# Loads of batch 1 ahead of its bits, and the output weights in two other slots, in a hash attention with SwiGLU on one Trainium2 core

## The chip, the cores and the metric

One NeuronCore of a Trainium2 chip runs the whole program. The metric is the device time of one execution in microseconds (us). A measurement gives several executions; their median is quoted, and one more execution is profiled.

## The reference: what is computed

Four batches of eight heads attend over 768 tokens of 64 numbers. A query sees only the keys whose six hash bits equal its own. The result goes, without a residual, through an RMS norm and a SwiGLU layer.

```python
q_bits = (einsum('bhsd,dk->bhsk', q, proj) > 0);  k_bits = (einsum(..., k, proj) > 0)
mask = q_bucket[:, :, :, None] == k_bucket[:, :, None, :]
scores = where(mask, scale * q @ k.T, -1e9)
attn = exp(scores - max);  attn = attn / (sum(attn) + 1e-9)
x = (attn @ v) laid out as 3072 tokens x 512
xn = x / sqrt(mean(x * x) + 1e-6) * rms_g
g, val = xn @ w_gate, xn @ w_val          # 512 x 1536 each
out = (g * sigmoid(g) * val) @ w_out      # 1536 x 512
```

## The kernel before, in words

**Tiles.** Heads are taken in pairs: (b, hp) is pair hp of batch b. The queries of a batch are halved, so that there are eight windows w of 384 queries, two to a batch. One score tile is one window, one head and a third of the keys (256): two matmuls of 128 keys by 384 queries in `scores` (L344). SLOTS (L35) lists the 192 of these tiles; slot s of the program prepares the scores of tile s + 1 and does the rest of what is due. Tiles 0 to 47 belong to batch 0, 48 to 95 to batch 1. The mask costs no instruction of its own: twelve rows of hash bits, with signs and weights, stand below the 64 rows of k and of q in the tile QK, so that one matmul adds the mask to the scores, and ACT's exp (L354) brings masked ones to zero.

**How a pair is prepared.** Its k, q and v come by DMA into tiles kL, qL and vL of a pool of ten buffers (`lpool`). In batch 0 and pair (1,0), k and q come as rows (`load_rows`, L112) and are turned by PE. In all other pairs they come as blocks (`load_blocks`, L122): four DMAs for k and four for q, each of 24 x 32 x 32 numbers in runs of 128 bytes. DVE turns them with four transposes each (L194, `turn_dve`), POOL casts them into QK (L202), PE multiplies them with the projection (L210, `d_ps`), DVE takes the signs (L217, `bits`), and DMAs of SP carry the bits into QK: eight DMAs for (1,0) (L268) and eight for each of (1,1) to (1,3) (L285); L303 does it for two pairs of later batches at a time. v is cast by POOL (L310) and summed by POOL (L316 to L318, `v_sum`).

**The feed-forward part.** When a window's eight heads are done it is normalised, turned (L431), multiplied by the gate weights (L446) and the value weights (L456), and by the output weights wo (L469, `project`). For window 0 the gate matmuls begin in slot 42 and the project matmuls in slot 58: slot 58 uses row blocks 0 to 3 of the twelve of wo, slot 59 blocks 4 to 7. The weights come by DMAs that POOL issues and that turn fp32 into fp16: gate and value weights in halves (L520), wo in two halves of six row blocks (`load_wo`, L526).

**What sets the order.** Everything is ordered by hand. `at(s, f, ...)` (L576) puts a step into slot s; inside a slot, steps go by rank and then in the order in which they were put there. The dictionary `work` (L636) gives for each pair the slots of its k, q and v load, the first of its eight turning slots and the slot of its hash. The casts follow four and eight slots after the first turn, v's cast and sum nine after it. A slot says only where an instruction stands in its engine's queue. SP's queue holds nothing but DMA issues: loads, bits and the stores of the result (L478). SP goes through it in order, and an issue that has to wait, for data or for an earlier DMA, holds all that stand behind it. POOL's queue holds the weight loads among its arithmetic.

**What the loads wait for.** Each load needs a free buffer of the ten, and each of SP's DMAs waits for the one eight places before it on the queue. The matmuls that make g_ps, v_ps, y_ps, x_ps, t_ps, m_ps and d_ps share three PSUM banks (`bank`, tag "g"), taken in the order of the program.

Of the kernel before, what the change touches and what calls it, by code (L numbers as in the profile page):

```python
# [44 lines left out]
def kernel(  # L45
# [530 lines left out]
    def at(s, f, *a, rank=3):  # L576
        plan[s].append((rank, len(plan[s]), lambda: f(*a)))
# [36 lines left out]
    for i, (t, src) in enumerate(((wg, moe_w_gate), (wv, moe_w_val))):  # L614
        at(2 + 4 * i, load_w, t, src, 0, 768)
        at(12 + 9 * i, load_w, t, src, 768, 1536)
        at(43 + 7 * i, load_wo, 6 * i, 6 * i + 6)


    for which, sl in zip("kqv", (9, 11, 15)):  # L620
# [12 lines left out]
    def in_row(loads, s, hash_slot=None):  # L633
        return loads, range(s, s + 8), (s + 4, s + 8, s + 9), hash_slot

    work = {  # L636
        (1, 1): in_row((21, 32, 33), 42, 51), (1, 2): in_row((38, 42, 44), 49, 58),
        (1, 3): in_row((46, 52, 54), 56, 65),
        (2, 0): in_row((56, 60, 62), 64), (2, 1): in_row((63, 66, 69), 72, 81),
        (2, 2): in_row((71, 75, 78), 81), (2, 3): in_row((80, 83, 86), 89, 98),  # L640
        (3, 0): in_row((90, 94, 98), 100), (3, 1): in_row((100, 104, 108), 110, 119),
        (3, 2): in_row((116, 120, 124), 126), (3, 3): in_row((126, 130, 134), 136, 145),
    }
# [120 lines left out]
```

## Time and profile before

| what | us |
|---|---|
| median of 3 runs (340.05 to 343.66) | 341.2 |
| the profiled execution | 340.95 |
| its span, first to last instruction | 339.2 |
| PE busy | 326.1 |
| DVE busy | 237.7 |
| ACT busy | 207.9 |
| POOL busy | 155.6 |

The profile shows one execution. A row of its timeline has the start in us from the beginning of the span, the duration, the engine, the line of the kernel, the operation, the tiles (out<-in) and how many instructions are merged; in brackets stands the idle time of the engine ahead of it and what ended it. SPq is SP's queue of DMA issues: the duration is that of issuing, not of the transfer. A row of a table by stretch gives, for PE, PEld (weight loads), DVE, ACT and POOL, the busy us and the count, then PEclk, the share of full clock that TensorE was granted, the share of time that the 16 DMA engines were busy and the GB/s moved. Queue q1 carries the DMAs of SP, q0 those of POOL.

### The profile page before, as it was taken

What the parts mean: (1) busy time and instruction counts of PE and PEld (TensorE: products, weight loads), DVE (VectorE), ACT (ScalarE), POOL (GpSimd) and SP (SyncE); (2) the same over time, 40 slices, a digit from 0 to 9 for tenths busy, and PEclk for the clock granted to TensorE, in tenths of its full rate; (3) what the DMA queues carried; (4) which work ended last, traced back from release to release, by engine and by line L of the source; (5) the groups of instructions that cost most, each with busy time, mean ns of one, the idle gap of its engine ahead of it and who ended that gap; (6) DMA issues with size and microseconds to landing.
All of it is one profiled execution on the core that took longest, in us unless ns stands there. A gap on an engine that the chain in (4) does not pass through costs nothing.

```text
span 339.2 us, 7797 instructions
## 1 busy us (share of the span) xinstructions
PE 326.1 (96%) x2983; PEld 200.2 (59%) x2983; DVE 237.7 (70%) x532; ACT 207.9 (61%) x324; POOL 155.6 (46%) x230
## 2 busy tenths in 40 slices
PE   8999989599989999999999999999999999999995
PEld 7566666265555655656565655656566655655653
DVE  4789669489587986978767794977356754784860
ACT  3789987356465755666665766666666766532321
POOL 4888766178745586374826156463101311130000
PEclk9999999989999999999999999999999999999999
DMA  7998929947273947605531572000110001001002
GB/s 236 334 231 192 140 50 183 175 79 135 44 177 78 199 56 178 109 9 119 124 82 24 109 121 90 22 12 7 38 56 2 3 31 64 2 1 62 33 0 93
DMA packets 85972, 31.36 MB, mean 92 GB/s; under 512 B 71480, under 2 KB 82992, under 8 KB 85936
## 3 DMA queue, kind: packets, MB, share of 16 engines
q1 hardware_dynamic: 82000, 26.09, 33.4%
q0 software_dynamic: 3712, 4.72, 8.8%
q8 instruction: 23, 0.38, 0.5%
q14 instruction: 13, 0.11, 0.1%
q10 hardware_dynamic: 224, 0.07, 0.1%
HBM read 28.32 MB, written 6.29 MB: 102 GB/s over the span
## 4 chain that ended last, share of the span: by engine, by line
PE 80%; DVE 8%; POOL 3%; DMA 3%; SPq 2%; issue 2%; ACT 1%; DVEq 0%; ACTq 0%; POOLq 0%
PE y_ps L469 18%; PE v_ps L456 16%; PE s_ps L344 14%; PE g_ps L446 13%; PE o_ps L366 8%; PE d_ps L210 4%; PE s_ps L446 3%; DMA kL<-in_k_dram 2%; PE x_ps L431 1%; SPq L122 1%; SPq L285 1%; PE z_ps L337 1%; PE t_ps L170 1%; DMA QK<-bits 1%; DVE t L457 1%
## 5 line engine op out<-in xcount | busy, mean ns | idle before, releaser
L354 ACT ACTIVATE psb<-s_ps 128x768 f16<-128x768 f32 x192 | 150.6, 809 | 33.5 <-PE s_ps L344 31.7
L344 PE MATMUL s_ps<-QK 76*128 76x384 f16 x384 | 93.7, 326 | 3.0 <-DMA QK<-bits 1.3
L456 PE MATMUL v_ps<-xnT,wv 128*128 128x384 f16 x384 | 78.7, 327 | 0.0
L469 PE MATMUL y_ps<-wo,ht 128*128 128x512 f16 x276 | 69.2, 379 | 0.1
L448 ACT ACTIVATE t<-g_ps 128x384 f32<-128x384 f32 x78 | 38.2, 490 | 48.0 <-PE g_ps L446 47.5
L457 DVE SCALAR_TENSOR_TENSOR t<-t,g_ps 128x384 f32<-128x384 f32 x78 | 42.7, 547 | 32.5 <-ACT t L448 32.1
L366 PEld LDWEIGHTS <-psb 128*128 128x128 f16 x1152 | 52.4, 98 | 22.0 <-issue 3.9
L446 PE MATMUL g_ps<-xnT,wg 128*128 128x384 f16 x312 | 63.5, 325 | 1.2 <-DVE xnT L432 0.6
L390 POOL TENSOR_TENSOR x<-otmp,rcp 128x384 f32<-128x384 f32 x31 | 25.9, 835 | 83.6 <-DVE rcp L386 83.1
L458 DVE SCALAR_TENSOR_TENSOR ht<-t,v_ps 128x384 f16<-128x384 f32 x96 | 53.2, 554 | 10.8 <-PE v_ps L456 1.5
L366 PE MATMUL o_ps<-vl,psb 128*128 128x65 f16 x1152 | 56.9, 194 | 0.0
L446 PEld LDWEIGHTS <-wg 128*128 128x128 f16 x384 | 36.1, 97 | 25.2 <-issue 1.7
L456 PEld LDWEIGHTS <-wv 128*128 128x128 f16 x384 | 36.4, 98 | 23.8 <-issue 0.9
L344 PEld LDWEIGHTS <-QK 76*128 76x128 f16 x384 | 31.3, 98 | 20.8 <-issue 8.2
L469 PEld LDWEIGHTS <-ht 128*128 128x128 f16 x276 | 25.9, 97 | 25.1 <-issue 1.5
L476 ACT COPY ysb<-y_ps 128x512 f32<-128x512 f32 x23 | 13.5, 586 | 25.3 <-PE y_ps L469 24.9
L402 POOL TENSOR_TENSOR sq<-x 128x384 f32<-128x384 f32 x31 | 25.7, 827 | 2.5
L432 DVE TENSOR_TENSOR xnT<-x_ps,gcol 128x512 f16<-128x512 f16 x24 | 16.2, 681 | 14.5 <-PE x_ps L431 14.5
L202 POOL CAST QK<-qT 64x768 f16<-64x768 f32 x22 | 18.2, 827 | 17.2 <-DVE qT L194 16.5
L194 DVE STREAM_TRANSPOSE kT<-kL 128x192 f32<-128x192 f32 x44 | 22.1, 516 | 4.3 <-issue 4.3
L381 DVE TENSOR_TENSOR otmp<-o_ps,cvb 128x390 f32<-128x390 f32 x32 | 17.9, 558 | 8.1 <-PE o_ps L366 8.0
L202 POOL CAST QK<-kT 64x768 f16<-64x768 f32 x22 | 18.2, 828 | 10.5 <-PE v_ps L456 4.1
(80 smaller groups left out, 301.7 us busy)
## 6 DMA issues: line engine op xcount, KB each, us to landing
vL<-in_v_dram SPq DMA_DIRECT2D x16, 384.0 KB
out_dram<-ysb SPq DMA_DIRECT2D x23, 256.0 KB
kL<-in_k_dram SPq DMA_DIRECT2D x44, 96.0 KB
qL<-in_q_dram SPq DMA_DIRECT2D x44, 96.0 KB
kL<-in_k_dram SPq DMA_DIRECT2D x4, 384.0 KB
qL<-in_q_dram SPq DMA_DIRECT2D x4, 384.0 KB
wg<-in_moe_w_gate_dram POOLq DMA_DIRECT2D x2, 768.0 KB, 7.2
wv<-in_moe_w_val_dram POOLq DMA_DIRECT2D x2, 768.0 KB, 8.4
```

The costliest lines, as they stand in the source:

```text
L202: nc.gpsimd.tensor_copy(QK[b, hp][0:64, hh, o : o + S], T0[b, hp, which][64 * hh : 64 * hh + 64, :])
L344: nc.tensor.matmul(ps[:, j, 0:HALF], k_cols(w // 2, h, 2 * p + j), q_cols(w, h), start=True, stop=True,)
L354: nc.scalar.activation(psb[w, h][:, p], sps.pop(g)[:, :, 0:HALF], AF.Exp, scale=ESCALE,)
L366: nc.tensor.matmul(o[:, c, hh, 0:65], psb[w, h][:, jt // 2, jt % 2, 128 * c : 128 * c + 128], vls[b % 2][:, h, v_chunk(b, h, jt), 0:65], s ...
L390: eng.tensor_mul(xd.rearrange("p c (h d) -> p c h d", h=2), tmp[:, :, :, 0:64], r.to_broadcast([128, 3, 2, 64]),)
L402: nc.gpsimd.tensor_mul(sq, xd, xd)
L446: nc.tensor.matmul(g, wg[:, kt, fs], xnT[w][:, kt], start=(kt == 0), stop=(kt == 3))
L448: nc.scalar.activation(t, g, AF.Tanh, scale=0.5)
L456: nc.tensor.matmul(vv, wv[:, kt, fs], xnT[w][:, kt], start=(kt == 0), stop=(kt == 3))
L457: nc.vector.scalar_tensor_tensor(out=t, in0=t, scalar=1.0, in1=g, op0=ALU.add, op1=ALU.mult)
L458: nc.vector.scalar_tensor_tensor(out=ht[w][:, ft], in0=t, scalar=0.5, in1=vv, op0=ALU.mult, op1=ALU.mult)
L469: nc.tensor.matmul(y, ht[w][:, ft, c * 128 : (c + 1) * 128], wo[:, ft, :], start=(ft == 0), stop=(ft == NF - 1),)
```

## The change

Only numbers of slots change.

```diff
-        at(43 + 7 * i, load_wo, 6 * i, 6 * i + 6)
+        at(31 + 21 * i, load_wo, 6 * i, 6 * i + 6)
...
-        (1, 1): in_row((21, 32, 33), 42, 51), (1, 2): in_row((38, 42, 44), 49, 58),
-        (1, 3): in_row((46, 52, 54), 56, 65),
-        (2, 0): in_row((56, 60, 62), 64), (2, 1): in_row((63, 66, 69), 72, 81),
-        (2, 2): in_row((71, 75, 78), 81), (2, 3): in_row((80, 83, 86), 89, 98),
+        (1, 1): in_row((21, 22, 32), 42, 51), (1, 2): in_row((32, 33, 37), 49, 58),
+        (1, 3): in_row((38, 40, 44), 56, 65),
+        (2, 0): in_row((53, 55, 58), 64), (2, 1): in_row((59, 62, 66), 72, 81),
+        (2, 2): in_row((68, 71, 75), 81), (2, 3): in_row((78, 82, 86), 89, 98),
```

The three numbers in brackets are the slots of the k, q and v load. The turning slots and the hash slots stay. The order of the loads among themselves stays too, so each takes the same buffer as before. On PE, DVE and ACT no instruction moves. What moves is on SP and POOL.

On SP, from the k of (1,1) to the bits of (1,1), the order before:

```order
21 L122 DMA kL<-in_k_dram 32x24x32 x4
22 L268 DMA QK<-bits 12x384 x8
23 L122 DMA qL<-in_q_dram 32x24x32 x4
24 L112 DMA vL<-in_v_dram 128x2x384
25 L122 DMA kL<-in_k_dram 32x24x32 x4
26 L122 DMA qL<-in_q_dram 32x24x32 x4
27 L112 DMA vL<-in_v_dram 128x2x384
28 L122 DMA kL<-in_k_dram 32x24x32 x4
29 L285 DMA QK<-bits 12x384 x8
```

and now:

```order
21 L122 DMA kL<-in_k_dram 32x24x32 x4
22 L122 DMA qL<-in_q_dram 32x24x32 x4
23 L268 DMA QK<-bits 12x384 x8
24 L112 DMA vL<-in_v_dram 128x2x384
25 L122 DMA kL<-in_k_dram 32x24x32 x4
26 L122 DMA qL<-in_q_dram 32x24x32 x4
27 L112 DMA vL<-in_v_dram 128x2x384
28 L122 DMA kL<-in_k_dram 32x24x32 x4
29 L122 DMA qL<-in_q_dram 32x24x32 x4
30 L112 DMA vL<-in_v_dram 128x2x384
31 L285 DMA QK<-bits 12x384 x8
```

The q of (1,1) has moved ahead of the bits of (1,0) (L268), and the q and v of (1,3) ahead of the bits of (1,1) (L285).

On SP behind the bits of (1,1), up to the bits of (1,3), the order before:

```order
30 L122 DMA qL<-in_q_dram 32x24x32 x4
31 L112 DMA vL<-in_v_dram 128x2x384
32 L122 DMA kL<-in_k_dram 32x24x32 x4
33 L285 DMA QK<-bits 12x384 x8
34 L122 DMA qL<-in_q_dram 32x24x32 x4
35 L478 DMA out_dram<-ysb 128x512
36 L112 DMA vL<-in_v_dram 128x2x384
37 L122 DMA kL<-in_k_dram 32x24x32 x4
38 L478 DMA out_dram<-ysb 128x512
39 L285 DMA QK<-bits 12x384 x8
```

and now:

```order
32 L122 DMA kL<-in_k_dram 32x24x32 x4
33 L122 DMA qL<-in_q_dram 32x24x32 x4
34 L285 DMA QK<-bits 12x384 x8
35 L112 DMA vL<-in_v_dram 128x2x384
36 L122 DMA kL<-in_k_dram 32x24x32 x4
37 L478 DMA out_dram<-ysb 128x512
38 L122 DMA qL<-in_q_dram 32x24x32 x4
39 L478 DMA out_dram<-ysb 128x512
40 L285 DMA QK<-bits 12x384 x8
```

Ahead of the bits of (1,2) (the first L285 row) stand now k and q of (2,0), where q and v of (1,3) and the k of (2,0) stood. Between these bits and those of (1,3) are still eleven DMAs; the q of (2,1) is there instead of the q of (2,0).

On POOL, the second half of wo (slot 52 instead of 50), a piece of the difference behind the casts of (1,1):

```order
 L402 TENSOR_TENSOR sq<-x 128x384
 L202 COPY QK<-kT 64x768 x2
-L526 DMA wo<-in_moe_w_out_dram 128x6x512
 L202 COPY QK<-qT 64x768 x2
 L390 TENSOR_TENSOR x<-otmp,rcp 128x3x128
```

and where it stands now, behind the sum of the v of (1,1):

```order
 L317 TENSOR_TENSOR vadd<-vadd 128x2x64
 L318 TENSOR_TENSOR vsum_110<-vadd 128x2x64
+L526 DMA wo<-in_moe_w_out_dram 128x6x512
 L202 COPY QK<-kT 64x768 x2
 L415 TENSOR_SCALAR ms<-ss 128x3
```

It has moved from ahead of the q casts of (1,1) to ahead of the k casts of (1,2). The first half moves from slot 43 to 31, where it stands behind the last casts of (1,0) and ahead of the norm of window 0 (L415).

## The prediction

> **What bounds the kernel now.** I read the page's head first, then the waits of PE from 50 to 110 us, then PE and DVE side by side at the longest of them, then the DMA issues ahead of it. The head, and the waits (us in total, times, longest):
>
> ```profile
> span 339.2 us, 7797 instructions
> PE 326.1 (96%) x2983; PEld 200.2 (59%) x2983; DVE 237.7 (70%) x532; ACT 207.9 (61%) x324; POOL 155.6 (46%) x230
> ...
> PE d_ps L210 <- DVE t L457: 3.5, 1, 3.5
> PE s_ps L344 <- DMA QK<-bits: 1.3, 2, 1.1
> PE g_ps L446 <- DVE t L457: 0.5, 1, 0.5
> ```
>
> PE is the bound: 326.1 of 339.2 us. A change of loads alone can win only what PE idles, or loses to its clock, and can lose only by making PE wait. The matmuls on both sides of the longest wait, and DVE's work there:
>
> ```profile
> 62.44 0.81 PE L446 MATMUL g_ps<-xnT,wg 128*128 128x384 f16 x4
> 66.73 0.56 PE L210 MATMUL d_ps<-kT,pk 128*32 128x384 f32 x1 [3.48 <-DVE t L457]
> ...
> 60.92 0.52 DVE L194 STREAM_TRANSPOSE qT<-qL 128x192 f32<-128x192 f32 x1
> 65.77 0.52 DVE L194 STREAM_TRANSPOSE kT<-kL 128x192 f32<-128x192 f32 x1 [4.33 <-issue]
> ```
>
> PE stands 3.48 us because the bank for slot 51's hash comes free only with a DVE L457, and that stands behind DVE's transpose of the k of (1,2), slot 49, which waited 4.33 us. "Issue" means that the page shows no releaser; the operand's load is the one left. Busy time by stretch (PE, PEld, DVE, ACT, POOL; then PEclk, DMA share, GB/s):
>
> ```profile
> 52.00:60.00 8.00, 8.00 (x75) 5.06 (x74) 7.55 (x19) 6.03 (x11) 4.30 (x6) 1.00 1.10 185
> 64.00:72.00 8.00, 5.27 (x33) 2.56 (x34) 5.02 (x12) 2.06 (x4) 3.66 (x5) 0.79 0.91 162
> 60.00:84.00 24.00, 20.52 (x179) 11.41 (x178) 17.67 (x40) 12.20 (x20) 14.37 (x19) 0.93 0.77 134
> 102.00:110.00 8.00, 7.54 (x68) 4.84 (x69) 5.52 (x12) 4.42 (x8) 4.33 (x6) 1.00 0.38 79
> ```
>
> After standing, PE's clock is 0.79 over 8 us: 0.21 x 8 = 1.7 us of its work lost. So one late load costs 3.5 + 1.7 = 5.2 us. Why it is late: the issues of SP and of POOL, the time that the two wo loads took to land, and what SP's queue q1 moved between 59 and 65 us (packets, MB, share):
>
> ```profile
> 46.95 2.71 SPq L122 DMA_DIRECT2D qL<-in_q_dram  x4
> 49.76 0.59 SPq L112 DMA_DIRECT2D vL<-in_v_dram  x1
> 50.45 8.08 SPq L122 DMA_DIRECT2D kL<-in_k_dram  x4
> ...
> 49.12 0.94 POOL L526 DMA_DIRECT2D wo<-in_moe_w_out_dram  x1
> 57.72 0.89 POOL L526 DMA_DIRECT2D wo<-in_moe_w_out_dram  x1
> ...
> DMA to landing us min/median/max: 7.6/8.6/9.6
> ...
> q1 hardware_dynamic: 1751, 0.22, 32.9%
> ```
>
> The four DMAs of a block load are issued in 2.71 us undisturbed, but in 8.08 while wo is under way, from 49.12 to between 65.3 and 67.3. In 6 us of that q1 moves 0.22 MB, 37 GB/s, where one block load is 4 x 96 KB = 0.39 MB. The k of (1,2) creeps beside both halves.
>
> **The change, part by part.** Slots are counted along PE's rows from the first gate matmul, which slot 42 issues.
>
> Loads of (1,1) to (1,3). The q of (1,1) goes from slot 32 to 22, ahead of the eight bits DMAs of (1,0), and the first wo half to slot 31, behind POOL's casts. Rows of SP, of POOL, the first scores on these bits (slot 47), and the first scores on the last bits of batch 1 (slot 71):
>
> ```profile
> 32.70 3.04 SPq L122 DMA_DIRECT2D kL<-in_k_dram  x4
> 40.68 6.17 SPq L268 DMA_DIRECT2D QK<-bits  x8
> 98.56 7.09 SPq L285 DMA_DIRECT2D QK<-bits  x8
> ...
> 43.54 0.19 POOL L415 TENSOR_SCALAR ms<-ss 128x3 f32<-128x3 f32 x1 [2.56 <-DVE ss L413]
> ...
> 55.87 0.33 PE L344 MATMUL s_ps<-QK 76*128 76x384 f16 x1
> 102.23 0.49 PE L344 MATMUL s_ps<-QK 76*128 76x384 f16 x2 [1.07 <-DMA QK<-bits]
> ```
>
> From 35.7 to 40.7 SP only waits for the bits, so four more issues of 0.68 us (2.71 / 4) cost it nothing. The wo half starts at 41.0, at the head of POOL's idle 2.56 us: its issue of 0.94 is hidden, and it lands by 41.0 + 9.6 = 50.6. The q load may creep beside it, and the bits behind q. At the worst the last bits are issued when wo lands, 50.6. From issue to use a bits DMA needs some 2 us: three are issued from 98.56 at 0.89 each, to 101.2, and the scores on them begin at 102.23. So they are there by 53, 3 us before 55.87: cost 0, and beyond that only the excess.
>
> Then v of (1,1) and k of (1,2) follow the bits, k from 47.5, at worst from 51.5, with no wo under way after 50.6. With 2.71 us of issue and 2 us to arrive k is there by 52 to 56. DVE wants it at 61.44. The wait of 4.33 goes, and with it PE's 3.5 and the clock's 1.7: **minus 5.2 us**. Late next on that path is DVE itself (below). The other loads up to v of (1,3), 11 issues of 0.6 to 0.7 us, end between 58 and 64, before DVE has the bits of (1,1) at about 65.
>
> Second wo half. It goes from slot 50 to 52, behind POOL's sum of the v of (1,1). Its new place on POOL is between these two, and the project matmuls of slot 59 need it:
>
> ```profile
> 68.19 0.82 POOL L390 TENSOR_TENSOR x<-otmp,rcp 128x384 f32<-128x384 f32 x1 [4.98 <-DVE rcp L386]
> 72.64 1.70 POOL L202 CAST QK<-kT 64x768 f16<-64x768 f32 x2
> ...
> 80.72 1.03 PE L469 MATMUL y_ps<-wo,ht 128*128 128x512 f16 x4
> ```
>
> POOL's stretch up to the cast lasts 4.45 us and begins 4.3 earlier, at 63.9, so wo is issued at 68.35 and lands between 75.95 (7.6) and 77.95 (9.6). Slot 59 reads row blocks 4 to 7; block 6 is the first of the second half, two matmuls behind 80.72 at 81.15, and 5.2 earlier that is 75.95. So **a new wait of 0 to 2.0 us**. I take 0.4, near the lower end: one of the halves took 7.6 although block loads crept beside both, as they will beside this one. The cast behind it comes 0.9 later; its reader is 13 slots off.
>
> For a stall of that length the clock matters. After the 1.07 us stall at 102 the clock stands at 1.00, after the one of 3.48 at 0.79; between them no row decides. The Trainium skill ("TensorE: Matmul & The Clock Gate", Part 1) halves the clock only after an idle window of some 3.4 us; by that, too, a wait of 2 us costs 2 us and the sum stays.
>
> Batch 2's loads and the bits. Ahead of the bits of (1,2) SP now has k and q of (2,0), 8 issues; between them and the bits of (1,3) are 11 issues as before, with q of (2,1) in place of q of (2,0). Rows of SP before, and the first scores on the bits of (1,2), slot 65:
>
> ```profile
> 83.81 6.28 SPq L285 DMA_DIRECT2D QK<-bits  x8
> ...
> 89.16 0.49 PE L344 MATMUL s_ps<-QK 76*128 76x384 f16 x2
> ```
>
> Bits of (1,1): ready near 65, issued until 72. Then k and q of (2,0): 5.5 us undisturbed, to 77.5; k stands until wo lands, so I take 79. The bits of (1,2) go from 79 instead of 83.81; three are issued by 81.4 and arrive by 82.8, for scores that come at 89.16 - 4.8 = 84.4: no wait. The eight end at 85.3; 11 issues of 0.67 us put the bits of (1,3) at 92.7 to 93.4 instead of 98.56. The first scores on them would come at 102.23 - 1.07 - 4.8 = 96.4; the 98.56 to 102.23 of before, 3.7 us, gives 96.4 to 97.1. So 0 to 0.7 of the 1.3 us for bits stays; I take 0.3: **minus 1.0 us**.
>
> DVE is the cover that thins: 17.67 us busy in the 24 from 60 to 84, which become 18.8, so 94%. PE idled 0.5 us for DVE once; I add 0.3.
>
> Sum: -5.2 + 0.4 - 1.0 + 0.3 = **-5.5 us**. The profiled execution took 340.95 us (span 339.2 and 1.75 around it), 0.25 below the runs' median of 341.2. 340.95 - 5.5 = 335.45; I say 335.5.
>
> **The rivals.**
>
> 1. The second wo half or the bits come late: the crowding only moves, from the k of (1,2) to the k and q of (2,0). The row at 37 GB/s says that the two queues slow each other. With 9.6 us to landing PE waits 2.0 instead of 0.4, and bits held to wo's end add up to 1: -5.5 + 1.6 + 1.0 = -2.9, so 338.0. Against it, the k of (2,0) is wanted only in slot 64. I give it 0.20. The Trainium skill ("DMA: Bandwidth & Descriptors", Issuing engines are not separate DMA queues) speaks for it: DMAs of all issuers run on the same 16 engines and interleave. By that rule the crowding stays whole wherever wo goes beside loads.
>
> 2. DVE becomes the bound from 62 to 80, and jams of PE's three banks return 2 to 3 us: 338. Against it, from 52 to 60 DVE is busy 7.55 of 8 us, 94%, and PE 8.00. 0.08.
>
> 3. Slower, by one mechanism: slot 59 waits for wo so long that the clock drops again. It decides when wo takes over 11.4 us to land, at which PE waits 3.5 from 75.95 and the 1.7 of the clock follow: the 5.2 are returned. At 13 us the time is 341 to 343. For it: block loads take turns with wo. Against it: the halves before, beside such loads, landed in at most 9.6. 0.07.
>
> 4. The change doesn't do what it says: DVE's 4.33 us was no load, and the stall stays: 341. Against it, SP's 8.08 us just ahead. 0.05.
>
> **How the numbers follow.** The forecast has 0.60, with a range of its own of 334 to 337 (wo 0 to 2, bits 0 to 0.7, DVE 0 to 0.5). About 1%, 3.4 us, is what a measurement can tell from no change; the bound is 337.8. Rivals 1 and 2 lie around 338, half below it: faster 0.60 + 0.15 = 0.75. Their other half, rival 4 less a little, and the mild end of 3 are within 1%: 0.17. Slower: 0.08. The range of 333.7 to 339.7 leaves out rivals 3 and 4 and a twentieth more.
>
> **What the profile after would show.** Right: DVE's kT of (1,2) without idle ahead of it near 61.4; hash matmuls right behind the g_ps of 62.44; PEclk 1.00 from 60 to 72; four k issues in some 2.7 us near 48; y_ps of slot 59 with under 1 us of idle; scores near 97 with hardly a wait for bits. Wrong: an idle PE of over 2 us near 76, a wait of over 1 us for bits in slot 47, 65 or 71, or the 3.48 us under another releaser.

## The result, and the profile after

| | median us | range | executions |
|---|---|---|---|
| before | 340.62 | 339.88 to 343.66 | 4 |
| changed | 335.27 | 334.87 to 336.02 | 4 |

The ratio is 0.9847, with a 95% interval of 0.9814 to 0.988: 1.5% less time. A ratio leaves out executions that lie over 1.5% above the fastest of their kernel. The profiled execution took 334.87 us against 340.95, and its span is 6.1 us shorter.

The head of the page, then the waits of PE from 50 to 110 us (us in total, times, longest):

```profile
span 333.1 us, 7797 instructions
PE 324.1 (97%) x2983; PEld 199.3 (60%) x2983; DVE 237.9 (71%) x532; ACT 207.8 (62%) x324; POOL 155.6 (47%) x230
...
PE g_ps L446 <- DVE t L457: 0.5, 1, 0.5
PE s_ps L344 <- DMA QK<-bits: 0.4, 1, 0.4
```

The wait of d_ps, 3.5 us, is no longer in the list, and the one for bits has gone from 1.3 to 0.4. PE's busy time fell by 2.0 us with the same 2983 matmuls, about the clock's 1.7 of the forecast. The place itself in the timeline, PE first and DVE below:

```profile
62.38 0.81 PE L446 MATMUL g_ps<-xnT,wg 128*128 128x384 f16 x4
63.12 0.51 PE L210 MATMUL d_ps<-kT,pk 128*32 128x384 f32 x1
...
61.23 0.54 DVE L194 STREAM_TRANSPOSE kT<-kL 128x192 f32<-128x192 f32 x1
```

DVE turns the k of (1,2) without a pause, at 61.23 instead of 65.77, and the hash matmuls follow g_ps directly. The busy time by stretch (PE, PEld, DVE, ACT, POOL, PEclk, DMA share, GB/s):

```profile
64.00:72.00 8.00, 8.00 (x79) 5.19 (x80) 7.36 (x18) 5.52 (x9) 7.52 (x11) 1.00 0.69 122
60.00:84.00 24.00, 23.93 (x226) 13.67 (x224) 21.60 (x49) 15.41 (x24) 18.89 (x25) 1.00 0.75 122
```

PE is full in both, and the clock of 0.79 is 1.00. PE's count from 64 to 72 us is 79 instead of 33. In the timeline, SP's queue and POOL's second wo load:

```profile
41.97 8.33 SPq L268 DMA_DIRECT2D QK<-bits  x8
...
50.96 2.83 SPq L122 DMA_DIRECT2D kL<-in_k_dram  x4
...
65.65 6.72 SPq L285 DMA_DIRECT2D QK<-bits  x8
72.47 3.61 SPq L122 DMA_DIRECT2D kL<-in_k_dram  x4
...
78.95 6.27 SPq L285 DMA_DIRECT2D QK<-bits  x8
...
92.91 7.05 SPq L285 DMA_DIRECT2D QK<-bits  x8
...
68.38 0.94 POOL L526 DMA_DIRECT2D wo<-in_moe_w_out_dram  x1
```

The time that the two wo loads took to land:

```profile
DMA to landing us min/median/max: 7.8/7.9/8.1
```

The second row of the queue is the gain: the k of (1,2) is issued in 2.83 us instead of 8.08, since no wo load is under way. That DVE waited for this k in the kernel before shows in the trace's marks of landing: the last of its four DMAs is there at 65.69, and DVE's transpose of it begins at 65.77. The two places where something could have been given back are the project matmuls of slot 59 and the scores of slot 71, in PE's timeline:

```profile
75.51 1.26 PE L469 MATMUL y_ps<-wo,ht 128*128 128x512 f16 x4
...
96.56 0.48 PE L344 MATMUL s_ps<-QK 76*128 76x384 f16 x2 [0.39 <-DMA QK<-bits]
```

The four y_ps took 1.26 us instead of 1.03. The page merges them into one row and shows no bracket, so the wait for the second wo half is the 0.2 us more.

### The profile page after: what moved, and what is told of

The parts are those of the page before. It is cut to its first block, busy times and chain, and to the rows that moved or that the text cites. A ratio compares the mean times of both kernels' runs of the same rounds, so it can differ in the third digit from the quotient of the medians.

```text
span 333.1 us, 7797 instructions
## 1 busy us (share of the span) xinstructions
PE 324.1 (97%) x2983; PEld 199.3 (60%) x2983; DVE 237.9 (71%) x532; ACT 207.8 (62%) x324; POOL 155.6 (47%) x230
## 4 chain that ended last, share of the span: by engine, by line
PE 83%; DVE 7%; DMA 4%; POOL 2%; ACT 1%; issue 1%; SPq 0%; DVEq 0%; POOLq 0%; ACTq 0%
PE y_ps L469 18%; PE v_ps L456 16%; PE s_ps L344 15%; PE g_ps L446 14%; PE o_ps L366 8%; PE d_ps L210 4%; PE s_ps L446 4%; DMA wo<-in_moe_w_out_dram 2%; DMA QK<-bits 2%; PE x_ps L431 1%; PE t_ps L170 1%; PE z_ps L337 1%; PE y_ps L721 1%; DVE t L457 1%; DVE otmp L381 1%
```

## The experiments

The theory on trial: one load that crept beside wo cost 5.2 us (3.5 of standing and 1.7 of clock), and both parts of the change are needed to take it away without a new wait. Its rival: one part alone does it, and the rest moves DMAs that were hidden. The runs came in three groups, each with runs of the kernel before on the same chip.

**1. Only the wo loads move.** Kernel before with one line changed; the loads of pairs stay.

```diff
-        at(43 + 7 * i, load_wo, 6 * i, 6 * i + 6)
+        at(31 + 21 * i, load_wo, 6 * i, 6 * i + 6)
```

> Only the two wo halves move (slots 31 and 52); the loads stay as before. Crowding theory: k of (1,2) is issued from about 50.4 as before, but in some 2.7 us instead of 8.1, and lands near 55, so DVE's wait of 4.33 us and PE's 3.48 go and PEclk from 64 to 72 is 1.00: 5 us less than before, 335 to 336. Queue theory (k of (1,2) was late because of its place on SP, behind the bits and the q of (1,1)): most of the wait stays, 339 to 341.

338.63 us (337.84 to 341.56), ratio 0.993 (0.9888 to 0.9971), less than half of the gain. The stall of d_ps is gone, as the crowding theory said, but its time of 335 to 336 is missed. In place of the stall, in the profiled execution (341.13 us, among the slowest of the ten), the last bits of batch 1 are late. SP's rows and the scores of slot 71 in the timeline:

```profile
57.72 4.40 SPq L122 DMA_DIRECT2D kL<-in_k_dram  x4
65.12 6.65 SPq L285 DMA_DIRECT2D QK<-bits  x8
...
96.52 6.19 SPq L285 DMA_DIRECT2D QK<-bits  x8
...
100.18 0.80 PE L344 MATMUL s_ps<-QK 76*128 76x384 f16 x2 [3.57 <-DMA QK<-bits]
```

The stretches around them (columns as above):

```profile
96.00:100.00 4.00, 0.61 (x4) 0.16 (x2) 1.98 (x5) 0.90 (x2) 1.64 (x2) 0.85 0.63 114
100.00:104.00 4.00, 3.82 (x20) 2.13 (x21) 0.56 (x1) 1.70 (x3) 2.68 (x4) 0.50 0.07 16
104.00:108.00 4.00, 4.00 (x31) 2.27 (x29) 2.81 (x6) 1.44 (x3) 0.00 (x0) 0.80 0.84 166
```

After the wait PE runs at half clock. The scores begin 3.66 us behind the start of these bits. In the kernel before it was 3.67 (98.56 to 102.23), in the changed one 3.65 (92.91 to 96.56): where PE waits there, SP's queue sets its time. SP stands idle from 62.12 to 65.12, ahead of the bits of (1,1), and has 28 issues between these bits and those of (1,3), which it starts 3.6 us later than in the changed kernel. The count explains little of the 3.6: the changed kernel has 27 issues there and starts the bits of (1,1) 0.5 us later. But its loads right behind these bits take 6.5 us for 8 issues instead of 9.0 for 9, beside the second wo half in both, and the rows after them are shorter by 1.7. Removing the early stall made PE meet the next late link.

**2. Only the loads of pairs move.** The changed kernel with the old wo slots.

```diff
-        at(31 + 21 * i, load_wo, 6 * i, 6 * i + 6)
+        at(43 + 7 * i, load_wo, 6 * i, 6 * i + 6)
```

> Only the loads move; the wo halves stay in slots 43 and 50. Queue theory: k of (1,2) is issued from 47.5 and lands by 52 to 58, the wait goes as in the changed kernel: 335 to 336. Crowding theory: the first half, under way from 51, catches k of (1,2) half done; it lands with that half, near 58, just in time for 61.4, but q of (1,2), wanted near 64.5, creeps beside the second half and lands by 65 to 67: a wait of DVE of 0 to 2 us, 335.5 to 338. If the crowding alone counts and the queue nothing, DVE waits as before: 340 to 341.

341.55 us (340.53 to 342.3), ratio 1.0003 (0.9971 to 1.0035): nothing. PE's waits for bits from 50 to 110 us:

```profile
PE s_ps L344 <- DMA QK<-bits: 5.4, 3, 2.9
```

The k of (1,2) on SP and the two longest of these waits, in the timeline:

```profile
50.14 8.08 SPq L122 DMA_DIRECT2D kL<-in_k_dram  x4
...
77.53 0.48 PE L344 MATMUL s_ps<-QK 76*128 76x384 f16 x2 [2.08 <-DMA QK<-bits]
89.32 0.48 PE L344 MATMUL s_ps<-QK 76*128 76x384 f16 x2 [2.88 <-DMA QK<-bits]
```

The stretches at and behind them:

```profile
76.00:80.00 4.00, 2.47 (x21) 1.40 (x22) 2.99 (x6) 1.30 (x2) 3.78 (x6) 1.00 0.06 14
80.00:84.00 4.00, 4.00 (x44) 2.54 (x43) 1.83 (x4) 2.52 (x5) 0.97 (x2) 1.00 0.54 85
88.00:92.00 4.00, 2.68 (x17) 0.99 (x18) 1.52 (x3) 0.81 (x1) 2.67 (x4) 0.80 0.07 16
92.00:96.00 4.00, 4.00 (x27) 2.15 (x26) 0.27 (x1) 1.04 (x3) 0.00 (x0) 0.78 0.72 155
```

Beside wo the loads creep as before, and the bits now stand behind more of them: three waits for bits, 5.4 us, in place of one for DVE. DVE waits only 0.8 us for the k of (1,2), instead of 4.33. So the time is near the 340 to 341 of the last theory, but not for its reason, and no theory had foreseen these waits. The clock falls behind the second (0.80 and 0.78) and not behind the first.

**3. The clock's part, first try.** Kernel before, with 40 small matmuls more ahead of the scores of tile 52, whose results nothing reads, so that PE isn't idle in the stall.

```diff
-        idle(ps[:, 0, HALF:512], {0: 8, 3: 6}.get(g, 0))
+        idle(ps[:, 0, HALF:512], {0: 8, 3: 6, 52: 40}.get(g, 0))
```

> The kernel before, with 40 filler matmuls on unused columns of a score bank ahead of slot 51's scores; loads and weights as before. The filler takes about 2.3 us of the 3.48 that PE stood. Theory that the stall costs its own length and then the clock: DVE's wait of 4.33 stays, the hash matmuls start at 66.7 as before, PE's idle time there falls to about 1.2 us, PEclk stays at 1.00 from 64 to 72, and the time falls by the clock's 1.7 us to about 339. Rival, that the slow clock lies beside a DVE that is the bound by then: no gain, 340 to 341. If the filler only delays PE: up to 2 us more, 342 to 343.

342.69 us (339.74 to 344.32), ratio 1.0029 (0.9988 to 1.0071): the 339 is missed. The hash matmuls waited 1.78 us instead of 3.48, and the clock stayed at 1.00 in the stretch that had 0.79:

```profile
64.00:72.00 8.00, 6.22 (x66) 3.66 (x64) 5.16 (x12) 3.20 (x5) 2.92 (x4) 1.00 1.00 177
```

But the profiled execution (344.27 us) then stood in slot 71, as the timeline shows:

```profile
104.26 0.48 PE L344 MATMUL s_ps<-QK 76*128 76x384 f16 x2 [3.38 <-POOL QK L202]
```

The row names a cast of POOL, but in the kernel before these scores begin ahead of that cast (102.23 against 102.83). They begin 2.79 us behind the start of the second of the bits DMAs (101.47), as in the changed kernel (93.78 to 96.56, 2.78), so PE waited for bits. These were issued from 100.06; PE stood 3.38 us, and from 104 to 108 its clock was 0.71. So the run doesn't price the clock. Its two executions with a mean clock of 1.00 took 339.74 and 340.01 us.

**4. The second wo half two slots earlier.** The changed kernel with wo in slots 31 and 50.

```diff
-        at(31 + 21 * i, load_wo, 6 * i, 6 * i + 6)
+        at(31 + 19 * i, load_wo, 6 * i, 6 * i + 6)
```

> The changed kernel with the second wo half in slot 50 again (31 and 50). Crowding theory: k of (1,2) has landed before that half starts at 57.7, so DVE's kT does not wait; k and q of (1,3) creep beside the half but are wanted from slot 56 on, near 70; the wait of slot 59 for wo (0.2 us) goes, k and q of (2,0) are no longer crowded, and the bits of (1,2) and (1,3) come some 1 us earlier, which takes the last 0.4 us wait for bits: 0.3 to 0.7 us less than the changed kernel, 334.6 to 335.0. Rival, that a half in slot 50 holds DVE whatever else: 338 to 340.

340.8 us (339.68 to 343.35), ratio 0.9997 (0.9967 to 1.0028): the expectation missed, and the whole gain is gone. The early stall is gone as well; what came is seen in the timeline of SP and PE:

```profile
59.82 7.22 SPq L122 DMA_DIRECT2D kL<-in_k_dram  x4
...
71.72 6.20 SPq L285 DMA_DIRECT2D QK<-bits  x8
...
83.61 6.70 SPq L285 DMA_DIRECT2D QK<-bits  x8
...
87.29 0.48 PE L344 MATMUL s_ps<-QK 76*128 76x384 f16 x2 [2.63 <-DMA QK<-bits]
```

and in the stretch behind that wait:

```profile
88.00:92.00 4.00, 4.00 (x25) 1.75 (x26) 1.79 (x3) 0.68 (x1) 0.92 (x2) 0.61 0.16 40
```

Wo now meets the k of (1,3), 7.22 us for four issues, and every later row of the queue slips: the bits of (1,1) start 6.1 us later than in the changed kernel, those of (1,2) 4.7. (Of the 6.1, 1.6 were there before this half began: the k of (1,2) was issued from 52.58 instead of 50.96.) Nobody waits for the late k here; the bits behind it on the queue are what PE pays for, and then the clock (0.61). The slot of the second half is thus worth as much as the whole change.

**5. Wo, and five issues moved into SP's idle time.** Experiment 1, with the q and v of (1,3) in slot 50, ahead of the bits of (1,1). All other loads are as before.

```diff
-        (1, 3): in_row((46, 52, 54), 56, 65),
+        (1, 3): in_row((46, 50, 50), 56, 65),
```

> The kernel of the first experiment (only the wo halves moved) with five more issues moved: q and v of (1,3) from slots 52 and 54 to 50, ahead of the bits of (1,1), into the 3 us that SP stood there. Theory that SP's serial chain of issues, up to the bits of (1,3), sets slot 71: these bits go from 96.52 to about 91, the wait of 3.57 us in slot 71 and the half clock behind it go, and the time is that of the changed kernel, 335 to 335.5, though the q of (1,1) and all loads of batch 2 stand as before. Rival, that every part of the change is needed for itself: it stays near 338.6.

334.6 us (334.47 to 336.61), ratio 0.9804 (0.9742 to 0.9866): all of the gain. The timeline of SP, from the moved q on, and of PE, in the profiled execution, the slowest of the four:

```profile
62.52 2.99 SPq L122 DMA_DIRECT2D qL<-in_q_dram  x4
...
66.30 6.20 SPq L285 DMA_DIRECT2D QK<-bits  x8
...
93.21 6.19 SPq L285 DMA_DIRECT2D QK<-bits  x8
...
78.42 0.59 PE L469 MATMUL y_ps<-wo,ht 128*128 128x512 f16 x2 [2.22 <-DMA wo<-in_moe_w_out_dram]
```

and the stretch around PE's wait:

```profile
72.00:80.00 8.00, 5.78 (x50) 2.81 (x49) 6.84 (x15) 3.17 (x5) 7.28 (x10) 1.00 0.85 134
```

The five issues fill the three idle microseconds; the bits of (1,1) start 1.2 us later than in experiment 1, those of (1,3) 3.3 earlier (the expectation had 5.5), and there is no wait for bits. What the profiled execution lost, it lost to wo, which landed in up to 9.9 us; the clock stayed at 1.00.

**6 to 8. What batch 2's slots are worth.** The changed kernel with batch 2's loads in their old slots; with one load of (2,1) behind v; and this last with the second wo half in slot 51.

```diff
 6:
-        (2, 0): in_row((53, 55, 58), 64), (2, 1): in_row((59, 62, 66), 72, 81),
-        (2, 2): in_row((68, 71, 75), 81), (2, 3): in_row((78, 82, 86), 89, 98),
+        (2, 0): in_row((56, 60, 62), 64), (2, 1): in_row((63, 66, 69), 72, 81),
+        (2, 2): in_row((71, 75, 78), 81), (2, 3): in_row((80, 83, 86), 89, 98),
 7 and 8:
-        (2, 0): in_row((53, 55, 58), 64), (2, 1): in_row((59, 62, 66), 72, 81),
+        (2, 0): in_row((53, 55, 58), 64), (2, 1): in_row((59, 66, 66), 72, 81),
 8:
-        at(31 + 21 * i, load_wo, 6 * i, 6 * i + 6)
+        at(31 + 20 * i, load_wo, 6 * i, 6 * i + 6)
```

> The changed kernel with the loads of batch 2 in their old slots. Four issues fewer stand ahead of the bits of (1,3) (q of (2,0) behind the bits of (1,2), q of (2,1) behind those of (1,3)). Chain theory: these bits are issued from about 90 instead of 92.91, the 0.39 us wait for them goes, 334.6 to 335.1; so the last part of the change brings nothing or costs a little. Rival, that batch 2's early loads are part of the gain: 336 to 338.

> The changed kernel with the q of (2,1) in slot 66 instead of 62, behind the bits of (1,3). Chain theory: bits of (1,3) from about 90.2 instead of 92.91, the 0.39 us wait of slot 71 goes, 334.7 to 335.1; the q is wanted from slot 76 on and has time. Rival, that the wait of slot 71 is not SP's order but something else late: no difference, 335.3.

> As the one before, and the second wo half in slot 51 instead of 52, ahead of the cast and sum of the v of (1,1) on POOL. It is issued near 65.6 instead of 68.4, lands near 73.6, so slot 59 no longer waits (0.23 us), and k and q of (2,0) are less crowded: 334.4 to 334.9. Crowding rival: the half now takes the bits of (1,1), wanted in slot 59 at 75.2, and makes them late: 336 to 340.

Experiment 6: 334.85 us (334.56 to 335.36), ratio 0.9799 (0.9743 to 0.9855). Experiment 7: 334.62 (334.51 to 336.74), 0.9811 (0.9737 to 0.9885). Both are where the chain theory had them, within 0.1 us. In both profiles the bits of (1,3) start earlier than in the changed kernel (91.81 and 91.29 against 92.91), and the one wait of PE that is left from 50 to 110 us is the 0.5 for DVE. Experiment 8: 334.43, 340.24, 340.14 and 337.12 us; the ratio, 0.9824 (0.9727 to 0.9922), is that of the first and the last alone. Its profile is that of the 334.43 and has the 0.5 for DVE alone, too. So the expected 334.4 to 334.9 came in one execution of four, and the crowding rival's 336 to 340 is not refuted. The two of 340 had a mean clock of 0.994 and 0.995, where the others had 1.00 (one stretch of 3.4 us at half clock in a span of 338 makes 0.995). No profile shows what held them.

**9. The stall by itself.** Experiment 6 with ten multiplications of a scratch tile on DVE ahead of the turning of (1,2): 4.55 us of work that nothing reads, with no DMA moved. The edit, without the lines that set up the tile `scr`:

```diff
+    def hold():
+        for _ in range(10):
+            nc.vector.tensor_mul(scr, scr, scr)
+
+    at(49, hold, rank=4.9)
```

> The changed kernel with batch 2's loads in their old slots, in which PE waits for no load and no bits, and ten scratch multiplications of 128 x 256 on DVE ahead of its transposes of slot 49: DVE is held some 4.3 us, as by the late load before, but nothing is late on SP. Theory that the early stall itself costs its length and the clock: hash matmuls start some 3.5 us late, PEclk drops behind them, the time is 5 us more than without, near 340. If PE makes up for it later because other work had to wait anyway: 335 to 337.

339.69 us (339.33 to 340.44), ratio 0.9963 (0.9946 to 0.998). DVE's hold and the stall in the timeline (the line numbers are one higher in this kernel):

```profile
61.07 4.55 DVE L667 TENSOR_TENSOR scr<-scr 128x256 f32<-128x256 f32 x10
...
66.83 0.85 PE L211 MATMUL d_ps<-kT,pk 128*32 128x384 f32 x1 [3.43 <-DVE t L458]
```

and the stretch:

```profile
64.00:72.00 8.00, 5.17 (x34) 2.34 (x35) 6.92 (x17) 2.23 (x4) 5.20 (x7) 0.79 0.46 100
```

It is the stall of the kernel before, made by hand: 3.43 us, and 0.79 over the same eight. The span is 337.7 against 332.8 for experiment 6, so the price is 4.9 us where nothing else waits. These are two executions on different chips; beside experiment 12, the same kernel without the hold on the same chip, the medians are 4.2 us apart (339.69 and 335.52).

**10. The clock's part, second try.** Experiment 9 with the 40 small matmuls of experiment 3.

> The same with 40 filler matmuls (2.3 us) on unused columns ahead of slot 51's scores, inside the time that PE would stand. If the slow clock behind the stall is a cost of its own, PEclk stays at 1.00 and the time falls by 1.7 us to about 338.3; if it is hidden beside DVE, no difference, 340.

338.95 us (338.52 to 340.26), ratio 0.9947 (0.9924 to 0.997): 0.74 less than experiment 9, not 1.7. The timeline has the added matmuls and what is left of the stall:

```profile
62.80 2.40 PE L338 MATMUL s_ps<-ones 128*128 128x128 f16 x40
...
67.39 0.51 PE L211 MATMUL d_ps<-kT,pk 128*32 128x384 f32 x1 [1.22 <-DVE t L458]
```

The stretch:

```profile
64.00:72.00 8.00, 6.78 (x74) 4.16 (x72) 7.51 (x19) 3.20 (x5) 4.72 (x6) 1.00 0.84 157
```

And a line of PE's waits from 50 to 110 us:

```profile
PE y_ps L470 <- DMA wo<-in_moe_w_out_dram: 0.7, 1, 0.7
```

The clock stays at 1.00. The profiled execution (339.53 us, 0.6 above the median) was as long as that of experiment 9 (339.51). It was 0.5 us late ahead of the added matmuls already (DVE's hold began at 61.61 instead of 61.07), and then it waited 0.7 us for wo, which experiment 9 didn't. That leaves 0.5 of the 1.7 unexplained in this pair; the clock's price is shown in part only. The kernel before gives a second view of it: of its 58 executions in these three groups, six had a mean clock of 1.00 and a median of 339.57 us (339.04 to 340.21), and the 52 at 0.995 or less one of 341.1. That is 1.5 us between them, though they may differ in other ways as well.

**11 and 12. The changed kernel and experiment 6 side by side,** unaltered, in five rounds on one chip.

> The changed kernel again, beside the one below on the same chip: 335.3.

> The changed kernel with batch 2's loads in their old slots again. Chain theory: 0.4 us less than the changed kernel beside it, 334.8 to 335.0. Rival, that the difference seen was noise: the same, 335.3.

The changed kernel took 337.02 us (335.04 to 337.89), ratio 0.9875 (0.9844 to 0.9906); the one with batch 2's old slots 335.52 (334.19 to 338.94), 0.9847 (0.9808 to 0.9887). The changed kernel is thus 1.7 us above the 335.3 expected, and its gain here 1.2% instead of 1.5; two of its six executions, and one of the other's, had a mean clock of 0.995. The medians are 1.5 us apart, but the intervals overlap. Where the profiled executions waited, the changed kernel first:

```profile
77.18 0.59 PE L469 MATMUL y_ps<-wo,ht 128*128 128x512 f16 x2 [0.98 <-DMA wo<-in_moe_w_out_dram]
98.19 0.48 PE L344 MATMUL s_ps<-QK 76*128 76x384 f16 x2 [1.00 <-DMA QK<-bits]
```

and with batch 2's old slots:

```profile
76.62 0.59 PE L469 MATMUL y_ps<-wo,ht 128*128 128x512 f16 x2 [0.39 <-DMA wo<-in_moe_w_out_dram]
```

So the new place of batch 2's loads brings nothing that these runs show, and may cost about a microsecond, which is not shown: the q of (2,1) stands ahead of the bits of (1,3), which started at 94.54 instead of 92.45 in these two profiles and were late by the 1.00 us.

## Why the prediction was right

It gave 335.5 us and a range of 333.7 to 339.7; the kernel took 335.27, and 337.02 when it was measured again. The steps came out as forecast in the main; that the first median is only 0.2 us off is partly luck.

- **The late load, minus 5.2.** Right in cause and size. The k came in time and stall and clock loss went together; experiment 9 made the same stall without any DMA and paid 4.9 (4.2 between the medians on one chip). The steps that lead there were too hopeful. The k of (1,2) was issued from 50.96 and not from 47.5, and in the second profile from 52.42, past the worst that I allowed (51.5). I had put the q of (1,1) ahead of the bits of (1,0) at no cost; it took 5.50 us to issue instead of 2.71 and put these bits back from 40.68 to 41.97, and beside the first wo half they took 8.33 instead of 6.17. The slack of 5 us absorbed it. The loads from there to the v of (1,3) are 14 issues and not 11; they ended at 65.55, not between 58 and 64, so that SP came to the bits of (1,1) with nothing to spare.
- **The second wo half, plus 0.4 within 0 to 2.0.** Issued at 68.38 (forecast 68.35); the wait was 0.2 in the first profile and 0.98 in the second of the same kernel. Its neighbours showed 0.39 and, in experiment 5, 2.22 with 9.9 us to landing. So the bounds hold but for 0.2 in that one, and where the wait falls between them changes from one execution to the next. The 9.6 us that I took for the slowest landing was passed twice, by 9.9 and, in experiment 10, 10.3. In rival 3 the sum is off: 11.4 us from 68.35 end at 79.75, a wait of 3.8 and not 3.5, which is reached at 11.1. No half landed so late.
- **The bits, minus 1.0.** Bits of (1,1) at 65.65 (forecast 65; held to the end by SP's loads), of (1,2) at 78.95 (79), of (1,3) at 92.91 (92.7 to 93.4), scores at 96.56 (96.4 to 97.1). The wait left was 0.39, within the forecast's 0 to 0.7; in the second profile it was 1.00, past it, with the bits of (1,3) at 94.54.
- **DVE, plus 0.3.** It didn't come. DVE is busy 21.60 of the 24 us from 60 to 84, 90% against the forecast's 94%, and PE is full there (23.93); its one wait for DVE is 0.5 us, as before.
- **The sum.** Minus 5.2, plus 0.2, minus 0.9 (1.3 to 0.4) is minus 5.9, and the span fell by 6.1 where minus 5.5 was forecast. Between the medians the gain was 5.35 us, and 3.94 in the second measurement (340.96 to 337.02), so the small error of the first is no measure of the forecast.

Of the rivals, the first came true in other kernels. "The crowding only moves" is what happened with either part alone (experiments 1 and 2) and with the second half in slot 50 (experiment 4). What the prediction did not see is how close by this lies. It spoke of minus 5.2 as the price of one late load, but taking away the load's delay alone gave 2.4 us, because the bits of (1,3) were 1.07 us behind PE with the stall in place, and up to 3.57 without it. The term for the bits was a condition for the first term, and not a small addition to it.

What stays open: the two executions of 340 in experiment 8; how much of the 5 us is the clock's; why wo takes 7.8 us to land in one execution and 9.9 in another; and why SP needs longer for an issue while another load is under way.

The kernels of experiments 5, 6 and 7 have medians of 334.6 to 334.85 us on one chip. None is shown to be faster than the changed kernel by more than the intervals, but experiment 6 does with half of the edit, and experiment 5 with four numbers.

## What to carry to other kernels

Where one queue issues loads and late-bound DMAs in order, a stall's price is not what its removal brings: work out when the next DMAs of that queue are issued and when the bound engine will then ask for them. First look for time in which the queue only waits, and move issues into it; here five issues moved into 3 us did with one wo edit what the whole change does. And place a large load from another queue where nothing that anybody waits for is issued beside it: here two slots made the difference between all of the gain and none.

## What the runs showed of the hardware

**A load on one queue slows another, and its issues too.** While the second wo half lands, the DMA queues of the changed kernel from 70 to 74.5 us (packets, MB, share of 16 engines; q0 is POOL's, q1 SP's):

```profile
q0 software_dynamic: 672, 0.69, 107.4%
q1 hardware_dynamic: 27, 0.01, 1.4%
```

The 0.01 MB overstates it: until 72.47 SP had issued only bits, DMAs of 9 KB. From there a block load was under way, and in its first 2.0 us the queue still moved 0.01 MB, where it moved 0.11 MB in the first 2.05 us of the q load of the kernel before (from 46.95 on, ahead of the first wo half). The clearer case is the kernel before itself, with 0.22 MB in 6 us beside wo's 0.79. There the issue itself is held: two issues of the k of (1,2) took 4.49 us (from 51.06) instead of 1.3. This is not the wait for the DMA eight places earlier, for the one that the second of them follows had landed by 47.97. I had taken such a transfer to slow the other; I had not reckoned that it holds the issues behind it as well, and so the bits that PE waits for.

**The clock falls after less idle time than 3.4 us.** Stalls of 3.48, 3.43 and 3.38 us were followed by half clock, but so were those of 2.88 (experiment 2) and 2.63 (experiment 4), for 3.4 us each: in experiment 2, 0.80 and 0.78 over 4 us each make (0.20 + 0.22) x 4 / 0.5 = 3.4. Stalls of 2.08 and 2.22 were followed by none. The prediction cited the Trainium skill ("TensorE: Matmul & The Clock Gate", Part 1), which speaks of an idle window of some 3.4 us; the length of the slow stretch agrees with such a window, but as a length of stall that one must stay below, 2.63 us contradicts it.

What decides can be read from the times at which the traces record a change of the clock. In all fourteen traces, whole multiples of 3.413 us lie between two changes: 18 in the kernel before from the clock's first rise to its fall, 25 in experiment 2, 24 in experiment 4. So the clock seems to be set anew once in each stretch of that length. Laid on this grid, up to 330 us, every stretch at whose end the clock fell has PE idle for 1.81 us or more (1.81 in experiment 4, 3.08 in the kernel before), and no other stretch at full clock has more than 1.78 (the first wait of experiment 3). By this it is the idle time within one stretch that counts, and not the length of the stall: the 2.22 us of experiment 5 lay across two stretches, 1.47 and 0.75. No run controls how a stall lies to the grid, so the 1.7 us for the clock may be a price that one execution pays and another doesn't. In experiment 1 the clock stayed at half for two such stretches, (0.15 + 0.50 + 0.20) x 4 / 0.5 = 6.8 us, of which the first 1.4 still lay in the stall of 3.57.
